# Whole 512-token products instead of half ones in the first segment of an attention and feed-forward kernel

## The chip, the cores and the metric

The kernel runs on one core of a Trainium2 chip. The metric is the device time of one execution in microseconds (us); several executions are taken, and their median counts. A profile of one execution is read beside it.

A core has several engines with instruction streams of their own, which work through their lists in order and wait for each other by semaphores: TensorE (PE, matrix products; its weight loads are listed as PEld), VectorE (DVE), ScalarE (ACT), GpSimd (POOL) and SyncE (SP, which here only issues transfers). TensorE writes its products to PSUM, a small memory of banks, from which VectorE and ScalarE fetch them.

## The reference

A layer norm of x feeds two branches that are summed with x: an attention with a memory over four segments of 512 tokens, and a feed-forward layer with SiLU. Cut to what matters:

```python
x = A_x                                    # 1 x 2048 x 512
xn = _layernorm(x, axis=-1)
return x + _A_ref(xn, A_wq, A_wk, A_wv, A_wo, A_beta) + _B_ref(xn, B_w1, B_w2)

def _A_ref(x, wq, wk, wv, wo, beta):       # 32 heads of 16, N = 4 segments of L = 512
    q, k, v = x @ wq, x @ wk, x @ wv       # split in heads and segments
    for s in range(N):
        logits = jnp.einsum('bhqd,bhkd->bhqk', qs, ks) * scale + mask
        p = _softmax(logits, axis=-1)
        a_dot = jnp.einsum('bhqk,bhkd->bhqd', p, vs)
        o = g * a_mem + (1.0 - g) * a_dot  # a_mem from the memory M, z of earlier segments
        M = M + jnp.einsum('bhld,bhle->bhde', phi(ks), vs)
    return o @ wo

def _B_ref(x, w1, w2):                     # 512 -> 1792 -> 512
    return silu(x @ w1) @ w2
```

## The kernel before

**Tiling.** A segment s has 512 tokens, which are four token tiles of 128. The normalised tokens lie transposed in `xnT`, with the 512 features in four blocks of 128 (`ki`) and the tokens along the free dimension. A product of q, k or of the first feed-forward layer ("h") makes one tile of 128 outputs for the 512 tokens of a segment: weights of 128 x 128 per `ki` stand in TensorE, the tokens stream past, and four `ki` are summed up in one PSUM bank. There are 4 such tiles of q, 4 of k and 14 of h in each segment.

**The order.** The order of all work is written out by hand in `ORDER` (lines 17 to 89) as a list of pieces. Each word is a piece: `k0.1.2` is part 2 of tile 1 of k in segment 0; `h0.3.1` is part 1 of tile 3 of h in segment 0; `ka0.0` copies k tile 0 from PSUM on ScalarE, `kf0.0` spreads its keys on VectorE and ScalarE, `qa0.0` copies q tile 0 on ScalarE; `ha` and `hv` (lines 492 and 497) make SiLU out of h; `S5` makes a batch of scores on TensorE and its exponential on ScalarE (lines 724 and 730); `E` and `O` weigh the values (line 791); `o`, `oc`, `od` and `oh` are products of the output. Every engine goes through its share of the list in this order. The 72 batches of scores use one buffer of four PSUM banks.

**The start.** The first line of the list brings the first segment in: `Nv0` to `Nv3` normalise the token tiles on VectorE, `X0.1` to `X3.1` transpose them on TensorE (line 845), `Xa0.1`, `Xa1.1`, `Xv2.1` and `Xv3.1` copy them to `xnT` on ScalarE and VectorE (line 851). Its end is

```
... X2.1 Xa1.1 k0.1.0 tb Nv3 X3.1 Xv2.1 k0.1.1 Xv3.1 vv0.0 odd omask k0.0.0 k0.0.1 k0.0.2 k0.0.3 ka0.0 fp0.0
q0.0.0 kf0.0 q0.0.1 q0.0.2 q0.0.3 k0.1.2 k0.1.3 q0.2.0 v0.2.0 qa0.0 xs5 ka0.1 kp0.1   then S0
```

**The products.** `product` (line 333) issues one matmul, or four of 32 output rows each where `narrow` is set, which depends on the pieces around it ("128\*128" and "128\*32" in the profile, lines 336 and 338). `dense` (line 353) makes a part of a tile of q, k or h. In segment 0 parts 0 and 1 do the columns 0 to 255, that is token tiles 0 and 1, and parts 2 and 3 the columns 256 to 511, with two `ki` in each part; so a tile has eight matmuls of 256 columns. In segment 1 `dense_mm` (line 345) makes a tile in four parts of one `ki` each over 512 columns; in segments 2 and 3 in two parts of two `ki`. `w_sb` in the profile stands for the feed-forward weights, `wk_sb` and `wq_sb` for those of k and q.

Of the kernel before, what the change touches and what calls it, by code (L numbers as in the profile page):

```python
# [93 lines left out]
def kernel(  # L94
# [225 lines left out]
    def bank(shape, dtype, name):  # L320
        return pp.tile(shape, dtype, name=name, tag="pb")
# [11 lines left out]
    def product(out, lhsT, rhs, start, stop):  # L333

        if not narrow[0]:
            return [nc.tensor.matmul(out, lhsT=lhsT, rhs=rhs, start=start, stop=stop, skip_group_check=True)]  # L336
        return [
            nc.tensor.matmul(  # L338
                out[c : c + 32], lhsT=lhsT[:, c : c + 32], rhs=rhs, start=start, stop=stop,
                tile_position=(0, c), skip_group_check=True,  # L340
            )
            for c in range(0, P, 32)
        ]

    def dense_mm(s, key, part, lhsT, rhs):

        parts = 4 if s < 2 else 2
        if part == 0:
            sts[s][key] = bank([P, L], F32, "ps")
        for ki in range(part * DT // parts, (part + 1) * DT // parts):  # L350
            product(sts[s][key][:, :], lhsT(ki), rhs(ki), ki == 0, ki == DT - 1)

    def dense(s, name, w_sb, i, part):

        if s == 0:
            if part == 0:
                sts[s][name, i] = bank([P, L], F32, "ps")
            cols = slice(part // 2 * L // 2, (part // 2 + 1) * L // 2)
            for ki in (0, 1) if part % 2 == 0 else (2, 3):
                product(  # L360
                    sts[s][name, i][:, cols], w_sb[:, ki, i * P : (i + 1) * P], xnT[:, ki, cols],
                    ki == 0, ki == DT - 1,
                )
            return
        dense_mm(
            s, (name, i), part, lambda ki: w_sb[:, ki, i * P : (i + 1) * P],
            lambda ki: xnT[:, ki, s * L : (s + 1) * L],
        )

    def k_mm(s, dt, part):  # L370
        dense(s, "k", wk_sb, dt, part)
# [23 lines left out]
    def q_mm(s, dt, part):  # L395
        dense(s, "q", wq_sb, dt, part)
# [88 lines left out]
    def h_mm(s, ft, part):  # L485
        if "hT" not in sts[s]:
            sts[s]["hT"] = hpool.tile([P, FT, L], BF16, name="hT", tag="hT")
        dense(s, "h", w1_sb, ft, part)
# [454 lines left out]
```

## Time and profile before

| | |
|---|---|
| median of 3 runs | 220.42 us (219.96 to 220.6) |
| the profiled execution's span, first to last instruction | 218.2 us |
| granted TensorE clock | 1.000 of full speed |
| matmuls, weight loads | 3982, 4006 |
| exponentials on ScalarE | 72 |
| read from HBM, written | 9.96 MB, 2.10 MB |

The profile tells, for one execution, when each instruction ran and what ended the idle time before it. Matmuls are pipelined: the profile shows each from its start to its modelled end, and the next may start while it is still under way. So the pace of a row of matmuls is read from their starts, and the duration of a row of n in the timeline is n - 1 paces and one full duration. In the timeline a row gives the start, the duration, the engine, the line, the operation, the tiles (out<-in), the shape and how many were merged; in brackets the idle time before it and what ended it. A group of instructions shows the busy time, the mean duration in ns and the idle time before them.

### The profile page before, as it was taken

How to read it: one execution, taken by the hardware profiler on the slowest of the kernel's cores; microseconds unless marked ns; L12 is line 12 of the kernel's file. 1: busy time of each engine (PE TensorE's matmuls, PEld its weight loads, DVE VectorE, ACT ScalarE, POOL GpSimd, SP SyncE). 2: the span in 40 equal slices, each digit the busy share in tenths (PEclk: the TensorE clock that was granted, in tenths of full speed). 3: DMA queues.
4: the chain of work that ended last, by engine and by line, in shares of the span. 5: the costliest groups of instructions: out<-in, count | busy, mean ns of one | idle time of the engine just before them, and what ended most of it. 6: DMA issues, size and time to landing. Idle time of an engine off the chain costs nothing.

```text
span 218.2 us, 9267 instructions
## 1 busy us (share of the span) xinstructions
PE 210.9 (97%) x3982; PEld 116.1 (53%) x4006; DVE 181.3 (83%) x370; ACT 184.1 (84%) x173; POOL 127.4 (58%) x203
## 2 busy tenths in 40 slices
PE   7899999999999999999999999999999999999994
PEld 7666656655544544455444545445464544465653
DVE  6899999999799899667979886887979897858844
ACT  3799999999999999999999999999989998942000
POOL 6067676789568984697766436962787473410000
PEclk9999999999999999999999999999999999999999
DMA  6996249322200430541125131420042120412223
GB/s 183 344 375 160 51 125 243 74 53 53 51 5 17 157 71 10 117 95 40 49 67 83 54 97 28 74 77 6 0 132 73 52 73 13 131 32 79 84 66 98
DMA packets 33273, 19.60 MB, mean 90 GB/s; under 512 B 14672, under 2 KB 33232, under 8 KB 33232
## 3 DMA queue, kind: packets, MB, share of 16 engines
q1 hardware_dynamic: 30608, 16.39, 28.7%
q10 hardware_dynamic: 2624, 2.62, 3.8%
q8 instruction: 31, 0.51, 1.0%
q14 instruction: 10, 0.08, 0.1%
HBM read 9.96 MB, written 2.10 MB: 55 GB/s over the span
## 4 chain that ended last, share of the span: by engine, by line
PE 92%; DMA 3%; ACT 2%; issue 1%; SPq 1%; DVE 0%
PE ps L336 26%; PE psO L338 17%; PE ps L338 16%; PE psS L724 11%; PE psO L336 9%; PE psV L791 8%; PE psS L338 4%; DMA wk_sb<-in_A_wk_dram 3%; ACT Pb L730 2%; PE psM L452 1%; SPq L169 0%; SPq L158 0%; PE ps L509 0%; ACT th L492 0%; DVE o_half L668 0%
## 5 line engine op out<-in xcount | busy, mean ns | idle before, releaser
L730 ACT ACTIVATE Pb<-psS 128x2048 bf16<-128x2048 f32 x72 | 135.2, 1878 | 4.7 <-PE psS L724 2.4
L744 POOL TENSOR_SCALAR_AFFINE_SELECT Pb<-Pb 128x512 bf16<-128x512 bf16 (+2 forms) x88 | 62.3, 718 | 22.4 <-ACT Pb L730 19.6
L497 DVE SCALAR_TENSOR_TENSOR hT<-th,ps 128x512 bf16<-128x512 bf16 x56 | 38.0, 682 | 10.1 <-ACT th L492 9.4
L744 POOL TENSOR_SCALAR_AFFINE_SELECT lows<-Pb 64x512 bf16<-64x512 bf16 (+1 forms) x40 | 24.3, 607 | 32.0 <-ACT Pb L730 24.9
L338 PE MATMUL psO<-w_sb,hT 128*32 128x512 bf16 (+2 forms) x696 | 41.4, 321 | 0.0
L336 PE MATMUL ps<-xnT,w_sb 128*128 128x512 bf16 (+1 forms) x177 | 35.9, 330 | 0.2 <-issue 0.2
L492 ACT ACTIVATE th<-ps 128x512 bf16<-128x512 f32 x56 | 33.0, 594 | 3.5 <-PE ps L338 3.1
L338 PEld LDWEIGHTS <-hT 128*32 128x32 bf16 x864 | 21.5, 96 | 14.6 <-issue 3.1
L338 PE MATMUL ps<-xnT,w_sb 128*32 128x512 bf16 (+1 forms) x408 | 24.8, 349 | 0.0
L724 PE MATMUL psS<-qT,k 32*128 32x64 bf16 (+3 forms) x512 | 23.0, 233 | 0.2
L336 PEld LDWEIGHTS <-w_sb 128*128 128x128 bf16 x178 | 16.4, 98 | 11.9 <-issue 1.2
L336 PE MATMUL psO<-w_sb,hT 128*128 128x512 bf16 (+2 forms) x82 | 20.5, 324 | 0.7 <-issue 0.6
L791 PEld LDWEIGHTS <-Vz 128*32 128x32 bf16 x768 | 16.1, 97 | 9.5 <-issue 0.6
L791 PE MATMUL psV<-Pb,Vz 128*32 128x448 bf16 (+7 forms) x512 | 21.0, 286 | 0.0
L724 PEld LDWEIGHTS <-k 32*128 32x128 bf16 x512 | 9.3, 92 | 21.2 <-issue 20.4
L336 PE MATMUL ps<-xnT,wk_sb 128*128 128x256 bf16 (+1 forms) x63 | 14.4, 326 | 0.4 <-DMA wk_sb<-in_A_wk_dram 0.2
L724 PE MATMUL psS<-qT,kT 16*128 16x448 bf16 (+3 forms) x256 | 14.7, 269 | 0.0
L338 PEld LDWEIGHTS <-w_sb 128*32 128x32 bf16 x408 | 10.3, 96 | 6.7 <-issue 1.7
L621 DVE SCALAR_TENSOR_TENSOR o_out<-psO,x_res 128x512 bf16<-128x512 f32 x14 | 9.4, 679 | 5.0 <-PE psO L338 3.9
L336 PEld LDWEIGHTS <-hT 128*128 128x128 bf16 x92 | 8.5, 98 | 9.6 <-issue 2.1
L828 DVE CAST odd<-psV 128x512 bf16<-128x512 f32 x16 | 11.0, 687 | 2.4 <-PE psV L791 2.4
L338 PE MATMUL psO<-wo_sb,oT 128*32 128x512 bf16 x140 | 12.8, 379 | 0.0
(112 smaller groups left out, 330.0 us busy)
## 6 DMA issues: line engine op xcount, KB each, us to landing
spr<-rz SPq DMA_DIRECT2D x56, 64.0 KB
x_res<-in_A_x_dram SPq DMA_DIRECT2D x16, 128.0 KB
out_dram<-o_out SPq DMA_DIRECT2D x15, 128.0 KB
w_sb<-in_B_w_dram SPq DMA_DIRECT2D x2, 896.0 KB
w_sb<-in_B_w_dram ACTq DMA_DIRECT2D x1, 1792.0 KB
x_hi<-in_A_x_dram SPq DMA_DIRECT2D x2, 512.0 KB
wv_sb<-in_A_wv_dram SPq DMA_DIRECT2D x2, 256.0 KB
wk_sb<-in_A_wk_dram SPq DMA_DIRECT2D x1, 512.0 KB
```

The source lines that it names most:

```text
L336: return [nc.tensor.matmul(out, lhsT=lhsT, rhs=rhs, start=start, stop=stop, skip_group_check=True)]
L338: nc.tensor.matmul(out[c : c + 32], lhsT=lhsT[:, c : c + 32], rhs=rhs, start=start, stop=stop, tile_position=(0, c), skip_group_check=True,)
L452: nc.tensor.matmul(psM[32 * g : 32 * g + 32, i, :].rearrange("p (r d) -> p r d", d=DH), lhsT=st["phiK", dt][:, j, 32 * g : 32 * g + 32], r ...
L492: nc.scalar.activation(out=th[:], in_=sts[s]["h", ft][:, :], func=AF.Tanh, scale=0.5)
L497: nc.vector.scalar_tensor_tensor(out=st["hT"][:, ft, :], in0=st.pop(("th", ft))[:], scalar=1.0, in1=st.pop(("h", ft))[:, :], op0=ALU.add, ...
L621: out = nc.vector.scalar_tensor_tensor(out=o_out[:], in0=st.pop(("psO", j)), scalar=0.5, in1=st["x", j][:], op0=ALU.mult, op1=ALU.add)
L724: nc.tensor.matmul(psS[:, g, c : c + q2 - q1], lhsT=keys[rows], rhs=st["qT"][rows, dt, q1:q2], start=True, stop=True, tile_position=(32 * ...
L730: exp = nc.scalar.activation(out=blocks(Pb, b).rearrange("p y g c -> p g y c"), in_=psS[:, :, :].rearrange("p g (y c) -> p g y c", c=BLOCK ...
L744: over[id(Pb)].append(nc.gpsimd.affine_select(out=out, in_=in_, compare_op=ALU.is_ge, fill=0.0, base=base, pattern=[[0, out.shape[1]], [1, ...
L791: nc.tensor.matmul(psV[32 * g : 32 * g + 32, q0 : q0 + nq].rearrange("p (y c) -> p y c", y=weights.shape[2]), lhsT=Vzs[s % 2][:, kt, 4 * d ...
L828: copy(out=odd[:], in_=sts[s].pop(("psV", 1))[:, :])
```

## The change

In segment 0 only tile 1 of k is still made in two halves of columns. All other tiles of k and q and all of h go the way of the other segments, with four parts of one `ki` each over all 512 tokens. The list of pieces is not changed, so each part stands where it stood.

```diff
+    HALVED = {("k", 1)}
+
     def dense(s, name, w_sb, i, part):
 
-        if s == 0:
+        if s == 0 and (name, i) in HALVED:
             if part == 0:
                 sts[s][name, i] = bank([P, L], F32, "ps")
             cols = slice(part // 2 * L // 2, (part // 2 + 1) * L // 2)
```

The tiles that are no longer halved go through this, which is there already:

```python
    def dense_mm(s, key, part, lhsT, rhs):
        parts = 4 if s < 2 else 2
        if part == 0:
            sts[s][key] = bank([P, L], F32, "ps")
        for ki in range(part * DT // parts, (part + 1) * DT // parts):
            product(sts[s][key][:, :], lhsT(ki), rhs(ki), ki == 0, ki == DT - 1)
```

## The prediction

> **What bounds the kernel now.** I read the page's engine shares, its chain and its costliest group first.
>
> ```profile
> span 218.2 us, 9267 instructions
> PE 210.9 (97%) x3982; PEld 116.1 (53%) x4006; DVE 181.3 (83%) x370; ACT 184.1 (84%) x173; POOL 127.4 (58%) x203
> ...
> PE 92%; DMA 3%; ACT 2%; issue 1%; SPq 1%; DVE 0%
> ...
> L730 ACT ACTIVATE Pb<-psS 128x2048 bf16<-128x2048 f32 x72 | 135.2, 1878 | 4.7 <-PE psS L724 2.4
> ```
>
> TensorE is 97% busy and holds 92% of the chain, so fewer matmuls look like time won. But a busy PE here contains short waits, because a matmul's modelled end lies well after the next one's start. So I looked at the clockwork behind it, the 72 exponentials of ScalarE (line 730). They share one score buffer: batch n+1 of scores (line 724) cannot start before exponential n is done. The timeline of ScalarE, the first exponentials, two spacings later on, and the last:
>
> ```profile
> 12.40 1.88 ACT L730 ACTIVATE Pb<-psS 128x2048 bf16<-128x2048 f32 x1
> 14.79 1.88 ACT L730 ACTIVATE Pb<-psS 128x2048 bf16<-128x2048 f32 x1
> ...
> 22.01 1.88 ACT L730 ACTIVATE Pb<-psS 128x2048 bf16<-128x2048 f32 x1
> 24.38 1.88 ACT L730 ACTIVATE Pb<-psS 128x2048 bf16<-128x2048 f32 x1
> ...
> 31.67 1.88 ACT L730 ACTIVATE Pb<-psS 128x2048 bf16<-128x2048 f32 x1
> 34.49 1.88 ACT L730 ACTIVATE Pb<-psS 128x2048 bf16<-128x2048 f32 x1
> ...
> 58.93 1.90 ACT L730 ACTIVATE Pb<-psS 128x2048 bf16<-128x2048 f32 x1
> ```
>
> Starts lie 2.37 us apart at the least (22.01 to 24.38): 1.88 for the exponential, and 0.49 for the scores' wait and first products. From the first exponential to the twentieth (58.93) there are 19 spacings and 46.53 us, against 19 x 2.37 = 45.03. So in this stretch ScalarE's cycle and TensorE's work are balanced: TensorE comes late by 1.5 us in all, and this is all that any saving on TensorE can bring there. When is it late? Two score batches in TensorE's timeline show both cases:
>
> ```profile
> 14.35 0.40 PE L724 MATMUL psS<-qT,k 32*128 32x64 bf16 x8
> ...
> 34.04 0.40 PE L724 MATMUL psS<-qT,k 32*128 32x192 bf16 x8
> ```
>
> The exponential of 12.40 ends at 14.28 and the scores follow after 0.07. The one of 31.67 ends at 33.55, and they follow after 0.49: there TensorE was late. Beyond this stretch the change touches nothing: the pieces of segment 0 that it rewrites stand before the twentieth score batch in the order list.
>
> **What is removed.** The groups of matmuls by shape, 256 columns wide:
>
> ```profile
> L336 PE MATMUL ps<-xnT,w_sb 128*128 128x256 bf16 x82 | 11.5, 273 | 0.0
> L336 PE MATMUL ps<-xnT,wk_sb 128*128 128x256 bf16 x32 | 5.0, 273 | 0.2 <-DMA wk_sb<-in_A_wk_dram 0.2
> L336 PE MATMUL ps<-xnT,wq_sb 128*128 128x256 bf16 x32 | 4.8, 273 | 0.0
> L338 PE MATMUL ps<-xnT,w_sb 128*32 128x256 bf16 x120 | 4.5, 273 | 0.0
> ...
> L336 PEld LDWEIGHTS <-w_sb 128*128 128x128 bf16 x178 | 16.4, 98 | 11.9 <-issue 1.2
> ```
>
> Only eight of the wk_sb ones (tile 1 of k) stay. A pair of 256-column matmuls with the same weights becomes one of 512: 82/2 = 41 pairs, 24/2 = 12 and 16 in full width, and 120/2/4 = 15 groups of four in the narrow form: 84 pairs in all. The columns streamed stay the same, so a pair is worth only the difference in pace. Both paces stand in the timeline:
>
> ```profile
> 10.11 1.04 PE L336 MATMUL ps<-xnT,wq_sb 128*128 128x256 bf16 x8
> ...
> 74.83 1.03 PE L336 MATMUL ps<-xnT,w_sb 128*128 128x512 bf16 x4
> ...
> 34.81 1.05 PE L338 MATMUL ps<-xnT,w_sb 128*32 128x256 bf16 x32
> ...
> 56.75 1.03 PE L338 MATMUL ps<-xnT,wq_sb 128*32 128x512 bf16 x16
> ...
> L336 PE MATMUL ps<-xnT,w_sb 128*128 128x512 bf16 x95 | 24.9, 379 | 0.2 <-issue 0.2
> ```
>
> Eight of 256 take 1.04 with one modelled duration of 0.273 at the end: (1.04 - 0.273)/7 = 0.1096 each, 0.219 a pair. Four of 512: (1.03 - 0.379)/3 = 0.217. So a pair is worth 2.4 ns in full width; the narrow groups give 2 x (1.05 - 0.273)/7 = 0.222 against 0.217. With the rounding of the rows I bound a pair between 0 and 5 ns and take 2.4, since the wide rows are the more numerous: 84 x 2.4 = 0.20 us of TensorE's stream. The removed weight loads, 98 ns each, are worth nothing: they lie under the 109 ns matmul before them, or the pace would not be 0.1096. That cover would be gone only if a load took longer than the matmul; at 98 of 109 ns it doesn't.
>
> Nine of the 84 pairs (four of k tile 0, four of q tile 0, one of q tile 2) lie before the first scores and are counted in the stall below; 75 x 2.4 = 0.18 remain for the 19 spacings. They count only where TensorE is late. Reading the spacings one by one against the floor, nearly all of those with such pieces are late by 10 to 30 ns or more, a few by nothing. Bounds 0 and 0.18; I take **0.15 us saved**.
>
> The Trainium skill, "TensorE: Matmul & The Clock Gate", section "Back-to-back issue gap", would promise more: in a stream of weight loads and matmuls it gives about 131 ns a matmul for 512 columns and about 81 for 128. On a straight line between them 256 columns would take an estimated 98, a pair 196, and 84 pairs would save an estimated 5.5 us of stream. This case's rows disagree: 512 columns take 217 ns here, in such a stream.
>
> **What is added: a wait.** A half product of columns 0 to 255 reads the normalised tokens of tiles 0 and 1 alone. A whole one reads all four tiles. In the order list the first pieces of k tile 0 stand just behind the copies of tiles 2 and 3 to xnT, which VectorE does (line 851):
>
> ```profile
> 8.34 0.42 DVE L851 COPY xnT<-ptr 128x512 bf16<-128x512 bf16 x1
> 9.19 0.42 DVE L851 COPY xnT<-ptr 128x512 bf16<-128x512 bf16 x1 [0.43 <-PE ptr L845]
> 9.53 0.68 DVE L406 CAST Vz<-ps 128x512 bf16<-128x512 f32 x1
> ...
> 8.99 0.82 PE L336 MATMUL ps<-xnT,wk_sb 128*128 128x256 bf16 x6
> ...
> 9.67 0.60 PE L336 MATMUL ps<-xnT,wk_sb 128*128 128x256 bf16 x4
> 10.11 0.49 PE L336 MATMUL ps<-xnT,wq_sb 128*128 128x256 bf16 x3
> ```
>
> The copy of tile 3 ends at 9.61. Before, TensorE spends the time until then on six half products: two of k tile 1 (8.99, 9.10) and four of k tile 0 (9.21 to 9.65). The other four of tile 0 start at 9.67, 0.06 after the copy, and q tile 0 follows at 10.11. After, the two of k tile 1 still run, since that tile stays halved; then TensorE has nothing until 9.67, and k tile 0 takes four of 0.216 from there: q tile 0 starts at 10.53. That is 10.53 - 10.11 = **0.43 us late**, with the 2.4 ns of its own pairs already in it. The copy itself comes no earlier or later, as the transposes that it waits for stand ahead of all this.
>
> Who is queued behind? The whole of TensorE, and, through k tile 0 and q tile 0, ScalarE's way to the first exponential:
>
> ```profile
> 10.30 0.58 ACT L376 CAST kT<-ps 128x512 bf16<-128x512 f32 x1 [0.58 <-PE ps L336]
> 10.92 0.51 ACT L393 ACTIVATE k<-kT,pm_even 128x256 bf16<-128x256 bf16 x1
> 11.34 0.56 ACT L399 CAST qT<-ps 128x512 bf16<-128x512 f32 x1
> ...
> L724 PEld LDWEIGHTS <-k 32*128 32x128 bf16 x512 | 9.3, 92 | 21.2 <-issue 20.4 <-ACT qT L399 0.3
> ...
> 11.95 0.21 PE L724 MATMUL psS<-qT,k 32*128 32x64 bf16 x4
> ```
>
> ScalarE sat idle for 0.58 before it got k tile 0, then works without a gap to the copy of q, for which the first scores wait. So the first scores move from 11.95 to 12.38, and the exponentials with them. Both clocks of the kernel, TensorE's list and ScalarE's cycle, then run 0.43 behind; only transfers issued at the start are not moved, and none is waited for after this point on TensorE. Bounds for this term: 0 (if later slack took it up) and 0.43 (nothing takes it up); I take 0.43, as no engine on the chain stands outside the shift.
>
> Nothing else moves: no transfer is added, SP's and POOL's queues keep their order, and the last matmul of a tile ends as before, so its reader is not delayed.
>
> **The sum.** +0.43 - 0.15 = **+0.28 us**. The profiled execution has a span of 218.2, so 218.5 after; the runs' median lies 2.2 above the span, so 220.42 + 0.28 = 220.70. That is +0.13%. What a measurement can tell from no change is 0.3%, or 0.66 us; the three runs before themselves differ by 0.64.
>
> **The rivals.**
> *The stall is hidden.* If the first scores were held by something else than q tile 0, the 0.43 would vanish and the saving stay: 220.42 - 0.15 = 220.27. Against it speaks the wait on ACT qT in the row of line 724; for it only that SP's loads at the start are not shifted.
> *The stall is longer, and the kernel slower.* The whole tile's first matmul could be held not by the copy of tile 3 but by the VectorE work behind it, the cast of v (9.53 to 10.21), if tile 0 of k needed the bank which that cast frees. Then it starts near 10.27, 0.60 later: +0.88, 221.30. It decides from a start of 10.05 on (0.38 later, 0.66 in all). Against it: a half product of that tile started at 9.21, before the cast.
> *The loads were paid for.* If each of the 69 full-width pairs freed a weight load of 98 ns, the stream would shorten by 6.8 us, of which the exponentials let 1.5 through: 220.42 + 0.43 - 1.5 = 219.35, faster by 0.5%. The pace of 0.1096 speaks against it. By the Trainium skill's figures in "Back-to-back issue gap" of "TensorE: Matmul & The Clock Gate" the saving of stream would meet the same cap of 1.5.
> *The change does not reach the pieces.* All k, q and first-layer pieces of segment 0 go through the one branch, so only a tile with index 1 of k could be affected otherwise; I give it nothing.
>
> **How the numbers follow.** Forecast 0.82, hidden stall 0.06, longer stall 0.09, paid loads 0.03. The predicted time is the forecast's, 220.70. Its own terms reach from 220.42 + 0.43 - 0.18 = 220.67 to 220.85, and the spread of the runs puts some 0.3 on either side; the range of 220.0 to 221.2 holds the forecast and the hidden stall and leaves the other two out. Within 0.3%: nearly all of the forecast and the hidden stall, 0.85; slower: the longer stall and a little of the forecast's edge, 0.11; faster: the paid loads and a rest, 0.04.
>
> **What would show it.** In TensorE's timeline, an idle time of about 0.46 after the two half products of k tile 1, ended by VectorE's copy to xnT, and q tile 0 starting near 10.53. The first exponential near 12.83 instead of 12.40. Single products of 512 columns at 216 ns. The twentieth exponential near 58.93 + 0.28 = 59.21, and from there on the same offset to the end. Wrong would be: a first exponential at 12.40 (hidden), or one after 13.2 (longer stall); or a twentieth that comes before 58.9, which would mean that pairs cost more than 5 ns.

## The result, and the profile after

The changed kernel takes 221.50 us (median of 8 runs, 220.49 to 221.94), the kernel before 220.31 (8 runs, 219.60 to 220.94). The ratio is 1.0053 with a 95% interval of 1.0035 to 1.0071, that is 0.77 to 1.56 us more. A second series of 12 runs gave 1.0035 (1.0012 to 1.0059). So the change makes the kernel slower by about a microsecond, where 0.28 was forecast and 221.2 was the end of the range.

The profiled execution of the changed kernel is the fastest of its eight, at 220.49 us. Its page, with the engines, the chain, the costliest group and the queue of the instruction fetches:

```profile
span 218.8 us, 9008 instructions
PE 210.8 (96%) x3853; PEld 107.8 (49%) x3877; DVE 181.5 (83%) x370; ACT 184.2 (84%) x173; POOL 127.5 (58%) x203
...
q8 instruction: 30, 0.49, 1.0%
...
PE 87%; ACT 6%; DMA 3%; issue 1%; SPq 1%; DVE 1%
...
L732 ACT ACTIVATE Pb<-psS 128x2048 bf16<-128x2048 f32 x72 | 135.3, 1878 | 4.7 <-PE psS L726 2.4
```

129 matmuls and as many weight loads are gone (3982 to 3853, 4006 to 3877), TensorE's busy time fell by 0.1 us, and the span grew from 218.2 to 218.8. The packets of q8, the queue that brings in instructions, fell from 31 to 30. Before, the line was

```profile
q8 instruction: 31, 0.51, 1.0%
```

and the prediction paid no attention to it.

The start, in the timelines of TensorE, VectorE and ScalarE (start, duration, engine, line, tiles, in brackets the idle time before and what ended it):

```profile
9.08 0.38 PE L336 MATMUL ps<-xnT,wk_sb 128*128 128x256 bf16 x2
...
9.76 1.02 PE L336 MATMUL ps<-xnT,wk_sb 128*128 128x512 bf16 x4 [0.30 <-DVE xnT L853]
10.62 1.03 PE L336 MATMUL ps<-xnT,wq_sb 128*128 128x512 bf16 x4
...
9.28 0.42 DVE L853 COPY xnT<-ptr 128x512 bf16<-128x512 bf16 x1 [0.48 <-PE ptr L847]
...
10.81 0.59 ACT L378 CAST kT<-ps 128x512 bf16<-128x512 f32 x1 [1.06 <-PE ps L336]
...
12.91 1.88 ACT L732 ACTIVATE Pb<-psS 128x2048 bf16<-128x2048 f32 x1
```

The stall stands where it was expected: after the two half products of k tile 1 (9.08) TensorE waits for the copy to xnT, which ends at 9.70, and k tile 0 begins at 9.76. The weights of k came 0.08 later in this execution than in the profile of before (the first product on them starts at 8.62 instead of 8.54). Counted from that product, the first exponential starts after 4.29 instead of 3.86: **0.43 us late**. ScalarE's idle time before it gets k tile 0 grew by 0.48.

From there to the end this one execution comes near the forecast: the last exponential starts 0.53 later than in the profile of before, where the forecast of 0.28 and the 0.08 of the weights would give 0.36. What makes the other seven slower is not in this profile, and the experiments had to find it.

### The profile page after: what moved, and what is told of

The parts are those of the page before. It is cut to its first block, busy times and chain, and to the rows that moved or that the text cites. A ratio compares the mean times of both kernels' runs of the same rounds, so it can differ in the third digit from the quotient of the medians.

```text
span 218.8 us, 9008 instructions
## 1 busy us (share of the span) xinstructions
PE 210.8 (96%) x3853; PEld 107.8 (49%) x3877; DVE 181.5 (83%) x370; ACT 184.2 (84%) x173; POOL 127.5 (58%) x203
## 4 chain that ended last, share of the span: by engine, by line
PE 87%; ACT 6%; DMA 3%; issue 1%; SPq 1%; DVE 1%
PE ps L336 22%; PE psO L338 17%; PE ps L338 16%; PE psS L726 10%; PE psO L336 9%; PE psV L793 8%; ACT Pb L732 4%; PE psS L338 4%; DMA wk_sb<-in_A_wk_dram 3%; PE psM L454 1%; ACT ex L425 1%; ACT kT L378 0%; ACT th L494 0%; SPq L169 0%; SPq L158 0%
## 5 line engine op out<-in xcount | busy, mean ns | idle before, releaser
L336 PE MATMUL ps<-xnT,w_sb 128*128 128x512 bf16 x134 | 35.5, 380 | 0.4 <-issue 0.3
L338 PE MATMUL ps<-xnT,w_sb 128*32 128x512 bf16 x348 | 24.8, 380 | 0.0
L336 PEld LDWEIGHTS <-w_sb 128*128 128x128 bf16 x137 | 12.5, 98 | 13.8 <-issue 1.2
L336 PE MATMUL ps<-xnT,wk_sb 128*128 128x512 bf16 (+1 forms) x51 | 14.3, 363 | 0.7 <-DVE xnT L853 0.3
L419 POOL TENSOR_SCALAR pos<-kT 128x512 bf16<-128x512 bf16 x12 | 8.3, 690 | 7.7 <-ACT kT L378 7.2
```

The costliest lines, as they stand in the source:

```text
L338: nc.tensor.matmul(out[c : c + 32], lhsT=lhsT[:, c : c + 32], rhs=rhs, start=start, stop=stop, tile_position=(0, c), skip_group_check=True,)
L419: nc.gpsimd.tensor_scalar(out=pos[:], in0=phi_src(s, of, dt), scalar1=3.0e38, scalar2=0.0, op0=ALU.min, op1=ALU.max)
```

## The experiments

Three theories stood against each other at first. *Theory 1*: the stall is all, and moves both clocks by 0.43. *Theory 2*: the joined products or the shorter list cost something more behind the first exponential. *Theory 3*: any shift of the start costs more than its own size. After the first four runs Theory 2 took a sharper form, *Theory F*: TensorE's instructions come in fetches of 16 KB, and the shorter list puts a fetch against a transfer that is waited for. That q8 carries TensorE's list is inferred from its count: 31 packets for 7988 matmuls and loads, 30 for 7730, 32 for the 8114 of a longer list below (before_pad126).

### The change again, the stall alone, the rest alone, a plain shift

`after_again` is the changed kernel. The three others:

```diff
 k0_halved_too, against the changed kernel
-    HALVED = {("k", 1)}
+    HALVED = {("k", 0), ("k", 1)}

 only_k0_whole, against the kernel before
-        if s == 0:
+        if s == 0 and (name, i) != ("k", 0):

 before_busy8, against the kernel before, in the list of pieces
- ... vv0.0 odd omask k0.0.0 ...
+ ... vv0.0 odd omask busy8 k0.0.0 ...
```

> The changed kernel once more, to see how far its time and the place of its late transfers vary. Theory 1 (the stall of 0.43 us at k tile 0 moves everything, the remaining loss is the spread of single executions): +0.3 to +0.6 us against the kernel before. Theory 2 (there is a second, lasting cost beside the stall, somewhere behind the first exponential): +0.8 to +1.5 us again.

> The change, but tile 0 of k stays in halves as well, so the stall at the start is taken away and 80 of the 84 pairs stay joined. Theory 1: first exponential at 12.40 as before, and a time of 0 to 0.2 us below the kernel before. Theory 2 (a cost of the joined products or of the shorter instruction list behind the first exponential): the first exponential at 12.40, but a time still 0.3 to 0.8 us above the kernel before.

> The kernel before with tile 0 of k alone made whole: the stall without the joined products. Theory 1: first exponential near 12.83, time +0.43 us, so a little more than the changed kernel's own shift. Theory 2 (joined products or shorter list): +0.43 us and no more, clearly below the changed kernel. Theory 3 (any shift of the start costs more than its size, since later transfers come late against it): the same as the changed kernel, +0.8 to +1.3 us.

> The kernel before with eight idle products of 128 columns put ahead of k tile 0, which fill about 0.43 us on TensorE and change nothing else: a shift of the start alone, no product joined, no wait added. Theories 1 and 2: first exponential near 12.83, time +0.43 us. Theory 3: +0.8 to +1.3 us, like the changed kernel.

| run | median, us | kernel before, us | ratio (95%) |
|---|---|---|---|
| after_again | 221.51 | 220.63 | 1.0035 (1.0012 to 1.0059) |
| k0_halved_too | 220.40 | 220.63 | 0.9983 (0.9958 to 1.0009) |
| only_k0_whole | 220.82 | 220.63 | 1.0013 (0.9989 to 1.0037) |
| before_busy8 | 221.31 | 220.63 | 1.0030 (1.0004 to 1.0057) |

With tile 0 of k in halves the loss is gone; with tile 0 alone made whole there is little of it (0.2 us by the medians, 0.8 at the upper end of the interval). In their profiles the two differ at the start as they should, in TensorE's timeline; first the one with the halves, then the one with the whole tile:

```profile
9.35 1.28 PE L336 MATMUL ps<-xnT,wk_sb 128*128 128x256 bf16 x10
10.47 1.03 PE L336 MATMUL ps<-xnT,wq_sb 128*128 128x512 bf16 x4
```

```profile
9.68 0.38 PE L336 MATMUL ps<-xnT,wk_sb 128*128 128x256 bf16 x2
10.36 1.02 PE L336 MATMUL ps<-xnT,wk_sb 128*128 128x512 bf16 x4 [0.30 <-DVE xnT L851]
```

Theory 1 explains only_k0_whole, but not why the changed kernel loses 0.7 us more than it (221.51 against 220.82 in the same series, though the two intervals overlap). Theory 3 would want only_k0_whole as slow as the changed kernel; by the medians it isn't. The plain shift of before_busy8 is nearly as slow as the changed kernel, which speaks the other way. But its list is 16 instructions longer, and its profile loses 1.19 us at one place, ScalarE's exponential 16 (the first is number 0), which follows number 15 by 3.62 instead of 2.43:

```profile
49.23 1.88 ACT L730 ACTIVATE Pb<-psS 128x2048 bf16<-128x2048 f32 x1
52.85 1.88 ACT L730 ACTIVATE Pb<-psS 128x2048 bf16<-128x2048 f32 x1 [1.25 <-PE ps L336]
```

The profile of `after_again`, an execution at the median of the changed kernel, has a step at the same place, which the first profile lacks. Exponentials 15 and 16 and TensorE's scores for number 16:

```profile
49.87 1.88 ACT L732 ACTIVATE Pb<-psS 128x2048 bf16<-128x2048 f32 x1
52.91 1.88 ACT L732 ACTIVATE Pb<-psS 128x2048 bf16<-128x2048 f32 x1 [0.67 <-PE psS L726]
...
51.84 0.40 PE L726 MATMUL psS<-qT,k 32*128 32x192 bf16 x8
52.17 1.04 PE L336 MATMUL ps<-xnT,wq_sb 128*128 128x512 bf16 x3
```

TensorE is done with the scores at 52.24 and goes on without a gap, but the exponential that waits for them starts at 52.91. In the profile of before, numbers 15 and 16 are

```profile
49.00 1.88 ACT L730 ACTIVATE Pb<-psS 128x2048 bf16<-128x2048 f32 x1
51.43 1.88 ACT L730 ACTIVATE Pb<-psS 128x2048 bf16<-128x2048 f32 x1
```

so the spacing is 2.43 there and 3.04 here: 0.61 us lost at one place. VectorE, which waits for the products of the memory at the same time, and SP, which is issuing a small transfer, are held up to the same moment:

```profile
52.78 0.23 DVE L466 COPY M<-psM 128x64 f32<-128x64 f32 x1 [0.20 <-PE psS L726]
...
49.06 1.21 SPq L859 DMA_TRANSPOSE xnT<-xn_t  x1
50.36 1.09 SPq L815 DMA_DIRECT2D zraw<-oraw  x2
51.54 1.76 SPq L815 DMA_DIRECT2D zraw<-odd  x2
```

The two last transfers take SP 1.04 in the profile of before, 1.76 here. What is different on the queues? The transposing transfer of token tile 11 (issued at 49.06) moves 512 packets of 256 bytes. The view of the transfers, over that stretch, has a fetch among them (queue, kind: packets, MB, share of 16 engines; it is over 100% here, as long packets of one queue overlap):

```profile
q1 hardware_dynamic: 505, 0.12, 143.7%
q8 instruction: 1, 0.02, 5.0%
```

In the kernel before the same stretch, from 49.30 to 50.25, is without one:

```profile
DMA packets 537, 0.13 MB, mean 138 GB/s; under 512 B 537, under 2 KB 537, under 8 KB 537
## 3 DMA queue, kind: packets, MB, share of 16 engines
q1 hardware_dynamic: 537, 0.13, 70.5%
```

By the trace's packets the fetch starts at 50.27 there, 0.02 after the last packet of the transposing transfer (49.37 to 50.25). In after_again it starts at 50.45, inside them, and they take from 50.25 to 52.20, with four packets of 1.2 to 1.3 us where 0.018 is usual. They end 0.76 us after the fetch has ended. Eight of the 19 profiles of this case have such packets of 0.8 us and more in this transfer, before_busy8 among them, and in all eight they end 0.76 to 0.81 after the fetch. So it is the fetch that holds them. The Trainium skill, "Runtime: NRT & Kernel Launch", section "Instruction fetch mechanics", says that instructions come in blocks of 16 KB, or 256 instructions, and that a block boundary is mostly hidden. The size agrees with the trace (16384 bytes in each of the 30 packets of q8); that it is hidden holds in this kernel only as long as no transfer that is waited for stands behind it. 258 instructions fewer are one fetch and two instructions. In before_busy8 the fetch starts at 49.74, also inside the transposing packets (49.60 to 51.81). In only_k0_whole, whose list is only eight instructions shorter than the kernel before, it starts at 51.22 with the last of them, and there is no step.

### Moving the fetches alone

If the place of the fetch is the cause, a few more TensorE instructions where TensorE is idle anyway must change the time. The warm-up products on zeros ahead of the first transpose are a place: m of the 44 are cut into four of 32 by 32 each, with m = 11, 21 and 32 in the changed kernel (66, 126 and 192 more instructions) and 21 in the kernel before.

```diff
     def keep_busy(n):
-        for i in range(n):
+        m = 11 if n == 44 else 0
+        for i in range(4 * m):
+            nc.tensor.matmul(
+                idle[0:32, 0:32], lhsT=zraw[:, 0:32], rhs=zraw[:, 0:32], start=True, stop=True, tile_position=(0, 0)
+            )
+        for i in range(n - m):
             nc.tensor.matmul(idle[:, 0:P], lhsT=zraw[:, 0:P], rhs=zraw[:, 0:P], start=True, stop=True)
```

> The changed kernel with 11 of the idle products of the warm-up cut into four narrow ones each: 66 more TensorE instructions in the same time, so all later instruction fetches (16 KB, 256 instructions each) come about a quarter of their spacing earlier against the work. Nothing else moves. Theory 1 (the stall alone): 221.5 us as the changed kernel. Theory F (part of the loss is that the shorter list puts a fetch against the transfers near 50 us): the time moves by 0.4 us or more in one of the three padded runs, down to +0.4 us over the kernel before, and the profile then shows no step between exponentials 14 and 17.

> The same with 126 more instructions, about half of a fetch's spacing. Theory 1: 221.5 us. Theory F: farthest from the collision near 50 us, so +0.3 to +0.6 us over the kernel before, unless a fetch meets another transfer that is waited for.

> The same with 192 more instructions, about three quarters of a spacing. Theory 1: 221.5 us. Theory F: differs from the unpadded kernel and from the other pads by 0.3 us or more in some direction.

> The kernel before with 126 more instructions in the warm-up, no product joined and no stall. Theory 1: as the kernel before, within 0.3 us. Theory F: may move by 0.3 to 0.8 us up, since its fetches leave the places that they have had.

| run | median, us | kernel before, us | ratio (95%) |
|---|---|---|---|
| after_pad66 | 220.48 | 220.36 | 1.0006 (0.9988 to 1.0023) |
| after_pad126 | 223.39 | 220.36 | 1.0125 (1.0096 to 1.0153) |
| after_pad192 | 222.40 | 220.36 | 1.0078 (1.0049 to 1.0108) |
| before_pad126 | 222.65 | 220.36 | 1.0115 (1.0076 to 1.0155) |

66 idle instructions take the loss away: the changed kernel with its stall is within 0.12 us of the kernel before by the medians (0.5 at the upper end of the interval, so there is room for the stall). In its profile the fetch near 50 us starts at 48.93, ahead of the transposing packets, and ends at 50.00. The packets (49.88 to 50.78) take as short as before, and the exponentials 14 to 16 run on without a step:

```profile
47.05 1.88 ACT L732 ACTIVATE Pb<-psS 128x2048 bf16<-128x2048 f32 x1
49.51 1.88 ACT L732 ACTIVATE Pb<-psS 128x2048 bf16<-128x2048 f32 x1
51.92 1.88 ACT L732 ACTIVATE Pb<-psS 128x2048 bf16<-128x2048 f32 x1
```

The two larger pads went against what I expected of them, +2 to +3 us, with and without the change. Most of their loss is at the start, where the first exponential comes at 14.83 to 16.01 instead of 12.40 (before) and 12.91 (after); with 126 more, another 0.8 (before_pad126) and 1.7 us (after_pad126) are lost behind the last exponential. The weights of k, for which TensorE waits until 8.54 in the kernel before, come about 2 us later, here in the timeline of after_pad126:

```profile
10.54 0.39 PE L336 MATMUL ps<-xnT,wk_sb 128*128 128x256 bf16 x2 [1.84 <-DMA wk_sb<-in_A_wk_dram]
```

The first fetch starts at 4.9 to 7.1 us in these three, in the midst of the weights' loading, where before and after the change it starts at 15.1 and 15.5, and with 66 more at 10.3. What else the narrow warm-up changes was not separated, so these three tell little of the changed kernel, except that more idle instructions at the start can cost microseconds.

### Moving the transfer instead

The other way round, TensorE's list stays and the transposing transfer moves, behind two pairs of small transfers:

```diff
 after_xd_late, against the changed kernel; before_xd_late, against the kernel before
- ... Nv11 XD11 E2 Ev2 O2 Ov2
+ ... Nv11 E2 Ev2 O2 Ov2 XD11
```

> The changed kernel, with the transfer that transposes token tile 11 (issued near 48.5 us) moved behind the next two pairs of row-sum transfers on SP's queue, some 3 us later. TensorE's list and its fetches stay as they are. Theory F (the fetch of 16 KB near 50 us runs into this transposing transfer, and what waits on it loses 0.6 us): no step of 0.6 between exponentials 14 and 17, and a time 0.5 to 0.8 us below the changed kernel, about +0.3 to +0.5 over the kernel before. Theory 1 (the stall alone): 221.5 us, as the changed kernel.

> The same move in the kernel before, as a control. Theory F: there the fetch falls just behind the transposing transfer, so the move brings nothing: within 0.3 us of the kernel before, or a loss if a fetch meets it at its new place. If the move by itself gained 0.5 us here too, Theory F's reading of the run above would fall.

| run | median, us | kernel before, us | ratio (95%) |
|---|---|---|---|
| after_xd_late | 220.82 | 220.29 | 1.0023 (1.0004 to 1.0043) |
| before_xd_late | 220.28 | 220.29 | 0.9998 (0.9983 to 1.0014) |

By the medians the changed kernel goes from 221.51 in the earlier series to 220.82 and is left with +0.5; the kernel before stays as it is. Counted from the kernel before in each series the gain is smaller, from 0.88 to 0.53, and the two intervals overlap. SP's timeline of after_xd_late shows the transfer at its new place, and the small ones back to their usual 1.08 and 1.04:

```profile
49.37 1.08 SPq L815 DMA_DIRECT2D zraw<-oraw  x2
50.54 1.04 SPq L815 DMA_DIRECT2D zraw<-odd  x2
51.63 1.22 SPq L859 DMA_TRANSPOSE xnT<-xn_t  x1
```

The fetch starts at 49.54 and finds no transposing packets to hold up, and there is no step between exponentials 14 and 17, as Theory F has it. The time leans the same way without settling it. The profiled execution, at 221.36 above the run's median, loses 0.81 at another place, exponential 66, of which more below.

### How often

The first profile of the changed kernel lacks the step, so it had to be seen how regular it is.

> One more profile of the changed kernel. Theory F: the fetch near 50 us starts inside the transposing transfer's packets, and the exponentials step by 0.5 us or more between 14 and 17; the time is near 221.5. Theory 1: no such step, and a time near 221.5 comes from another place.

> The changed kernel once more: Theory F expects the step in most of these looks, and a time near 220.7 in one that lacks it.

> The changed kernel a third time: Theory F expects the step in most of these looks, and a time near 220.7 in one that lacks it.

> One more profile of the kernel before. Theory F: the fetch near 50 us starts at the end of the transposing transfer's packets or behind them, and there is no step of 0.5 us between exponentials 14 and 17.

The last column is the span without the time up to the first exponential, which takes the stall and the arrival of the weights out:

| profile | us | fetch near 50 us starts | transposing packets, first to last start | steps | span - first exponential |
|---|---|---|---|---|---|
| before | 219.96 (inferred) | 50.27 | 49.37 to 50.25 | none | 218.2 - 12.40 = 205.8 |
| before_look1 | 220.38 | 50.58 | 49.80 to 50.57 | none | 218.7 - 12.82 = 205.9 |
| after | 220.49 | 49.40 | 49.82 to 51.50 | none over 0.11 | 218.8 - 12.91 = 205.9 |
| after_again | 221.50 | 50.45 | 50.25 to 52.20 | 0.61 at number 16 | 219.8 - 13.37 = 206.4 |
| after_look1 | 221.89 | 49.99 | 50.32 to 51.89 | 0.21 at 16, 0.76 at 66 | 220.2 - 13.44 = 206.8 |
| after_look2 | 221.17 | 49.32 | 49.58 to 51.16 | 0.22 at 16, 0.81 at 66 | 219.5 - 12.68 = 206.8 |
| after_look3 | 220.66 | 49.68 | 50.09 to 51.93 | none over 0.05 | 218.9 - 13.19 = 205.7 |

The time of the first row is inferred: in every other profile the time is 1.7 above the span, and of the three times on record 219.96 alone fits. In both profiles of before the fetch starts just behind the last packet, as if it had queued for it; in all five of the changed kernel it is under way among them, and they take 1.6 to 2.0 us instead of 0.8 to 0.9. In three of five the exponentials lose 0.2 to 0.6 there. In the other two SP bears it in the transposing issue itself, and no one waits; its timeline in the first profile of the changed kernel:

```profile
48.64 2.50 SPq L859 DMA_TRANSPOSE xnT<-xn_t  x1
```

against 1.21 in the profile of before. So the expectation of a step of 0.5 in most profiles failed: it came in one profile of five, and 0.2 in two. Those two lose more at another place, exponential 66. There VectorE's multiplication waits longer for the row factors (spr), in after_look2 and, for comparison, in the kernel before:

```profile
174.38 0.42 DVE L591 TENSOR_TENSOR oT<-spr,oraw 128x512 bf16<-128x512 bf16 x1 [0.86 <-DMA spr<-rz]
...
178.55 1.88 ACT L732 ACTIVATE Pb<-psS 128x2048 bf16<-128x2048 f32 x1 [0.45 <-PE psS L726]
```

```profile
173.57 0.42 DVE L589 TENSOR_TENSOR oT<-spr,oraw 128x512 bf16<-128x512 bf16 x1 [0.45 <-DMA spr<-rz]
```

0.41 more of waiting becomes 0.8 at the exponential. SP issued these transfers at the same distance to the work as before, so they were slow on the way. The trace's packets show what slowed them: again a fetch. The transfer of the row factors has 128 packets of 512 bytes. In after_look2 a fetch lasts from 171.35 to 172.77; 112 of the packets start by 171.82, and the last 16 only from 172.75 on. In the profile of before, 16 packets wait for a fetch in the same way (170.86 to 171.96, and from 171.94 on), but that fetch ends 0.5 ahead of exponential 64 instead of 0.1, and the wait of 0.45 costs the exponentials nothing. Of the 19 profiles, eight have 16 packets of this transfer held so, and in seven of the eight the first of them starts 0.01 to 0.02 before the fetch ends. Five of the eight have the step at 66, after_xd_late among them, all with the shorter list and no pad.

Against the work this fetch has not been moved by the change: it starts 1.1 to 1.6 us ahead of exponential 64 in all seven profiles of the table, as one would expect where 258 instructions fewer are nearly one whole fetch. It holds the transfer in four of the seven and misses it in three. Why the step at 66 is found only with the shorter list (five of its nine profiles without a pad, none of the five with the longer list and no pad) is not shown.

The first profile of the changed kernel has another, smaller wait for spr, of 0.36 at 80.64, which the profile of before has not; behind it exponential 29 loses 0.11.

### Versions without the stall

`k0_halved_xd_late` is, its name aside, k0_halved_too a second time, without the move. `k0_halved_pad66` and `k0_halved_xd_moved` are k0_halved_too with the pad and with the move shown above.

> The changed kernel with tile 0 of k in halves too, a second time: 0.1 to 0.4 us below the kernel before by both theories, as measured the first time, with a step near exponential 16 in few executions.

> Tile 0 of k in halves too, and the 66 more instructions in the warm-up: the stall taken away and the fetch near 50 us moved. Theory F and Theory 1: 0.43 us below the changed kernel with the same pad, so 0.1 to 0.4 us below the kernel before.

> Tile 0 of k in halves too, and the transposing transfer of tile 11 moved back as in after_xd_late: neither the stall at the start nor the step near 50 us, with 80 pairs joined. Theory F: the joined products' own saving of 0.1 to 0.2 us is what is left, so 0 to 0.3 us below the kernel before, unless the late landing near 173 us comes in (then up to 0.8 above in such executions).

| run | median, us | kernel before, us | ratio (95%) |
|---|---|---|---|
| k0_halved_xd_late | 220.46 | 220.29 | 1.0012 (0.9983 to 1.0040) |
| k0_halved_pad66 | 220.36 | 220.29 | 0.9999 (0.9981 to 1.0018) |
| k0_halved_xd_moved | 220.18 | 220.39 | 0.9992 (0.9971 to 1.0013) |

Without the stall no version differs from the kernel before by what these measurements can tell. The expectation for k0_halved_pad66, 0.43 below the changed kernel with the same pad, was missed: by the medians it is 0.12 (220.36 against 220.48, in two series), which neither confirms nor excludes the 0.43. The last one has the lowest median, 0.2 below, which is what the joined products were to save; the interval does not settle it. Its profile shows 217.9 - 12.12 = 205.8 from the first exponential on, no step over 0.05. Both profiles of k0_halved_too, of executions at 221.50 and 221.89, have steps of 0.6 at 16 and 0.7 to 0.9 at 66. So the steps need no stall. But these executions lie a microsecond above that kernel's medians (220.40 and 220.46), so most of its executions presumably do without them. By the medians, taking away the stall alone saves 1.1 us (221.51 to 220.40), the whole loss, and moving the fetches alone by 66 instructions saves 1.0 (to 220.48). The two losses are thus not independent; why the steps would come more often with the stall was not tried.

## Why the prediction was wrong

**The stall: right, to the hundredth.** Where, behind what, and 0.43 us: from the first product of k to the first exponential 4.29 instead of 3.86, in all five profiles of the changed kernel. The profile of only_k0_whole shows it alone (4.29), that of k0_halved_too is without it (3.86). What it is worth in time no run isolates that well: only_k0_whole is 0.2 us slower by the medians, with an interval from -0.2 to 0.8. The sign for the longer stall, a first exponential after 13.2, was badly chosen: it came in two of the five profiles (13.37 and 13.44) by a late arrival of the first weights.

**Nothing takes it up: right.** Counted from the first product of k, the last exponential starts 0.32 to 1.35 later than in the profile of before in the five profiles; 0.32 is the 0.43 less the saving below.

**The saving of the joined products: right in size up to number 14, then partly undone.** 512 columns in 216 ns, 0.15 foreseen; in the first profile after the change the exponentials' shift falls from 0.51 to 0.40 between numbers 0 and 14, 0.11 saved, and two small waits (0.05 at 15, 0.11 at 29) then undo it. In after_look3, which has no larger step, 0.1 is left at the end. (The prediction's two paces differ by 2.1 ns a pair as its rows give them, not 2.4, which changes nothing.) The rival in which the loads were paid for fell with the pace, and so did the 131 ns of the Trainium skill's section "Back-to-back issue gap" (page "TensorE: Matmul & The Clock Gate"): four of 512 take 1.03 here too.

**"Nothing else moves: no transfer is added, SP's and POOL's queues keep their order": wrong, and this is the step that failed.** It put the cost of the moved instruction fetches at nothing. TensorE's instructions come as transfers too, one fetch of 16 KB in some 7 us, and each lasts about 1 us where a packet of the transposing transfer takes 0.018. A list shorter by 258 instructions is shorter by one fetch, and the fetch near 50 us, which in the kernel before just misses the transposing transfer, runs into it in all five profiles of the changed kernel. In the mean of the five the step there costs 0.2 us. A second step, at exponential 66, costs 0.3 in the mean; it comes from a fetch too, but from one that the change has not moved against the work, and why it costs time only with the shorter list is open. I read the 1% of q8 on the page of before as nothing. It should have been a rival.

**The sum, set right.** From the table above, the changed kernel's five profiles are at 206.3 in the mean behind the first exponential, those of before at 205.85: 0.47 more. With the 0.43 of the stall this is 0.90, inside both measured intervals (0.77 to 1.56, and 0.26 to 1.30 from the second series). It is a sum over five executions, not a division of the loss between two causes that could be taken away one by one: taking away either the stall or the place of the fetches took nearly all of it. The rival of a longer stall gave nearly the measured time, 221.30, by a mechanism that didn't occur: the cast of v held nothing up. That would have been luck.

**The range** allowed 0.3 for the spread of single executions, from the three runs shown, and took one profile as the kernel. That profile was of a fast execution, the 219.96 among the three, so the 2.2 between span and median was 1.7 and a spread of 0.5. The later series of the kernel before run from 219.6 to 222.3; the arrival of the first weights alone differs by 0.4 between its two profiles (8.54 and 8.96).

## What to carry to other kernels

Before joining half products to whole ones, ask which half could run on what is already there: here one tile of eight half products covered a copy, and making it whole cost 0.43 us for a saving of 0.01. And where an instruction list gets longer or shorter by hundreds of instructions, its fetches move against every transfer: read the instruction queue's packets beside the transfers that are waited for, take several profiles, and try a few idle instructions more before a loss or a gain of half a microsecond is put down to the edit itself.

## What the runs showed of the hardware that was not expected

A fetch of 16 KB takes 0.9 to 1.6 us (570 of the 579 in the 19 profiles; the longest, 2.25, while the first weights load). Packets of the transposing transfer that it holds take up to 1.6 us (before_busy8) and end 0.76 to 0.81 after it; 16 of the 128 packets of the row factors wait until it has ended. Over the 19 profiles, 82 of the 87 issues on SP that took at least 0.4 us longer than the median of their kind (after the first 14 us) overlap a fetch, where of all such issues in the two profiles of the kernel before only 100 of 354 do. When the fetch met the transposing transfer in after_again, even a signal from TensorE to ScalarE came 0.6 us late, while TensorE worked on. The Trainium skill, "DMA: Bandwidth & Descriptors", section "Queues, rings and completion order", has a rule that fits the late landings: a transfer's semaphore write lands only after every earlier write of the same DMA engine, across its queues. The held packets that end 0.76 to 0.81 after a fetch agree with it, but no run tests it. Why an engine's own signal should wait with them, no run here shows.
